# Where load tiles start in SBUF, one product per denominator, and a finer last load in a decode-attention kernel

## Chip, cores and metric

The kernel runs on one core of a Trainium2 chip. The metric is device time in microseconds, median of several executions. A ratio is the mean time of one kernel's fast runs over that of the kernel before in the same rounds on the same chip, so not quite the ratio of the medians beside it; its interval is 95%. "The span's time" counts from the start of the profiled span, which is about 2 us shorter than the device time.

In profile lines, PE is TensorE's products and PEld its weight loads, DVE is VectorE, ACT ScalarE, POOL GpSimd, SPq the queue that issues the loads, DMA the 16 transfer engines. A timeline line gives start, duration, engine, source line (L), operation, out<-in, and in brackets the idle time before it and what ended it. A packet is one piece of a load, moved by one transfer engine. A stream of packets is called flat when they all take the usual shortest time, and a packet raised when it takes a little more.

## The reference, cut to what matters

A decode step: one token for each of two batch entries, layer-normed, goes through sliding-window attention (16 query heads on 8 key/value heads, window 4096, head size 256) and a small dense block with a mish activation; both are added to the input.

```python
W = min(4096, max(256, Sk // 4))                      # 4096 of 32768 positions
q = (x @ wq).reshape(B, Sq, Hq, Dh).transpose(0, 2, 1, 3)
k = repeat(k_cache[:, :, Sk - W:, :], rep, axis=1)    # rep = 2
v = repeat(v_cache[:, :, Sk - W:, :], rep, axis=1)
p = softmax(einsum("bhqd,bhkd->bhqk", q, k) * Dh ** -0.5)
o = einsum("bhqk,bhkd->bhqd", p, v)
return x + o.reshape(B, Sq, Hq * Dh) @ wo + mish_block(xn, w1, b1, w2)
```

There are 16 pairs of key/value head and batch entry. For each, 2 MiB of keys and 2 MiB of values are read once; all loads are 77.66 MB.

## The kernel before

The pools stand in SBUF in the order in which they are opened, so what `consts` holds sets where the load tiles start:

```python
consts = ctx.enter_context(tc.tile_pool(name="consts", bufs=1))
wo_pool = ctx.enter_context(tc.tile_pool(name="wo", bufs=3))
k_pool = ctx.enter_context(tc.tile_pool(name="kk", bufs=4))
v_pool = ctx.enter_context(tc.tile_pool(name="vv", bufs=5))
kt_pool = ctx.enter_context(tc.tile_pool(name="kt", bufs=3))
```

In the built program every tile of wo, k, v and kt starts 352 bytes past a multiple of 512. A key or value tile takes 16,384 contiguous bytes per partition. The denominators, and the main loop:

```python
def turn_p(s):                       # transpose the probabilities of step s; two steps per pair
    ...
    den = ps_den.tile([P, rep], FP32, tag="den", name="den")
    for n in range(NH):              # NH = 2
        nc.tensor.matmul(den[:], lhsT=rs[:, n : n + 1].to_broadcast([P, P]),
                         rhs=hsel[:], start=(n == 0), stop=(n == NH - 1))
    nc.vector.reciprocal(out=state["rec", i][:], in_=den[:])
...
for i in range(NK + KA):             # NK = 16 pairs, values two pairs behind
    if i + 2 < NK: load_k(i + 2)
    if i < NK:
        load_v(i, parts=1 if i < NK - 1 else 2)
        ...                          # load_wo at every second pair
        for half in range(NH):
            turn(s + 1)              # VectorE transposes keys into kt
            scores(s)                # TensorE products, ScalarE exp
            turn_p(s - 1)
    ...
    if i >= KA: values(i - KA)       # and mix(), the output product, at every second pair
```

The softmax here doesn't subtract the row's maximum and nothing guards it: scores larger than these inputs give would overflow.

## Time and profile before

| | before |
|---|---|
| device time, median | 194.75 us (194.56 to 195.1, 4 runs) |
| span profiled | 192.7 us |
| first load's data begins, last load's data ends | 1.79 and 187.87 us of the span |
| data packets' time per transfer engine (sum over 16) | 184.75 us |

The page shows one thing full: the transfer engines. The lines that say so, and those of the tail, stand in the prediction. The last two rows of the table come from the trace's records of single packets (start, duration, bytes). The sum (184.75) and the distance between first and last (186.08) are nearly equal: the stream has hardly a hole, so its length follows the sum of the packets. The sum is a mean over 16 engines, and the slowest of them ends later than the mean.

### The profile page before, as it was taken

How to read it: one execution, taken by the hardware profiler on the slowest of the kernel's cores; microseconds unless marked ns; L12 is line 12 of the kernel's file. 1: busy time of each engine (PE TensorE's matmuls, PEld its weight loads, DVE VectorE, ACT ScalarE, POOL GpSimd, SP SyncE). 2: the span in 40 equal slices, each digit the busy share in tenths (PEclk: the TensorE clock that was granted, in tenths of full speed). 3: DMA queues.
4: the chain of work that ended last, by engine and by line, in shares of the span. 5: the costliest groups of instructions: out<-in, count | busy, mean ns of one | idle time of the engine just before them, and what ended most of it. 6: DMA issues, size and time to landing. Idle time of an engine off the chain costs nothing.

```text
span 192.7 us, 3810 instructions
## 1 busy us (share of the span) xinstructions
PE 130.4 (68%) x1624; PEld 81.3 (42%) x1624; DVE 102.2 (53%) x137; ACT 25.5 (13%) x69; POOL 24.8 (13%) x138
## 2 busy tenths in 40 slices
PE   0242993999827985499709881797449592898854
PEld 0142381466513654246504651364324452364752
DVE  4605506996638390929264753838091744748101
ACT  5000110112200211012200220021101110021100
POOL 7004320022110112002200210020200200000000
PEclk9999996699995799669975998599957979589965
DMA  6999999999999999999999999999999999999960
GB/s 211 424 447 408 427 427 435 428 435 402 431 422 428 425 415 428 435 418 414 429 425 432 420 416 430 428 425 411 428 432 428 403 434 422 432 414 429 410 253 2
DMA packets 7674, 77.90 MB, mean 404 GB/s; under 512 B 741, under 2 KB 2793, under 8 KB 3050
## 3 DMA queue, kind: packets, MB, share of 16 engines
q1 hardware_dynamic: 7652, 77.66, 96.1%
q8 instruction: 12, 0.20, 0.4%
q14 instruction: 4, 0.03, 0.0%
q10 hardware_dynamic: 6, 0.01, 0.0%
HBM read 77.67 MB, written 0.00 MB: 403 GB/s over the span
## 4 chain that ended last, share of the span: by engine, by line
DMA 96%; PE 1%; SPq 1%; issue 0%; ACT 0%; DVE 0%
DMA v<-in_A_v_cache_dram 51%; DMA k<-in_A_k_cache_dram 18%; DMA wo<-in_A_wo_dram 17%; DMA v<-in_B_w_dram 10%; PE psA L201 1%; PE o L411 1%; SPq L109 0%; SPq L325 0%; ACT res L484 0%; DVE oT L422 0%; SPq L336 0%
## 5 line engine op out<-in xcount | busy, mean ns | idle before, releaser
L352 DVE STREAM_TRANSPOSE kt<-k 128x2048 f32<-128x2048 f32 x32 | 73.5, 2300 | 48.9 <-DMA k<-in_A_k_cache_dram 48.9
L364 PE MATMUL sc<-kt,qdiag 128*128 128x512 bf16 x256 | 75.0, 443 | 14.4 <-DVE kt L352 14.3
L364 PEld LDWEIGHTS <-qdiag 128*128 128x128 bf16 x256 | 26.1, 111 | 50.5 <-issue 24.1
L374 ACT ACTIVATE p<-sc 128x512 bf16<-128x512 f32 x32 | 19.1, 597 | 144.8 <-PE sc L364 140.9
L244 POOL COPY qdiag<-qrep 32x8 bf16<-32x8 bf16 x128 | 21.0, 186 | 125.3 <-PE sc L364 109.8
L201 PE MATMUL psA<-wo,oT 128*2 128x224 bf16 x64 | 12.5, 370 | 31.3 <-DVE oT L422 31.3
L411 PEld LDWEIGHTS <-v 128*128 128x128 bf16 x1024 | 27.9, 97 | 6.3 <-DMA v<-in_A_v_cache_dram 3.0
L411 PE MATMUL o<-pT,v 128*128 128x2 bf16 x1024 | 28.1, 163 | 2.7 <-DMA v<-in_A_v_cache_dram 2.7
L385 DVE STREAM_TRANSPOSE pT<-p 128x512 bf16<-128x512 bf16 x32 | 21.4, 671 | 0.0
L201 PEld LDWEIGHTS <-oT 128*2 128x2 bf16 x64 | 6.5, 111 | 34.6 <-DVE oT L422 32.0
L393 PEld LDWEIGHTS den<-hsel,rs 128*128 128x128 f32 x64 | 11.7, 227 | 3.8 <-issue 2.1
L401 DVE RECIPROCAL rec<-den 128x2 f32<-128x2 f32 x16 | 2.5, 153 | 18.7 <-PE den L393 18.7
L393 PE MATMUL den<-hsel,rs 128*128 128x2 f32 x64 | 9.4, 252 | 0.0
L215 PE MATMUL qT_ps<-xs,v 128*128 128x4 bf16 x112 | 3.3, 166 | 6.1 <-DMA v<-in_A_wq_dram 6.1
L422 DVE TENSOR_TENSOR oT<-o,rec 128x4 bf16<-128x4 f32 x16 | 2.1, 134 | 8.5 <-PE o L411 8.5
L374 ACT ACTIVATION_READ_ACCUMULATOR p<-sc 128x1 f32 x32 | 6.2, 194 | 0.0
L215 PEld LDWEIGHTS <-v 128*128 128x128 bf16 x112 | 3.1, 104 | 6.6 <-DMA v<-in_A_wq_dram 6.6
L224 DVE CAST qT<-qT_ps 128x64 bf16<-128x64 f32 x1 | 0.2, 225 | 7.0 <-PE qT_ps L215 7.0
L169 PE MATMUL xnT_ps<-ident,xn_bf 2*128 2x2 bf16 x7 | 0.5, 166 | 5.0 <-DVE xn_bf L133 5.0
L270 PE MATMUL hT_ps<-xs,v 128*128 128x4 bf16 x49 | 3.7, 195 | 0.0
L270 PEld LDWEIGHTS <-v 128*128 128x128 bf16 x49 | 3.2, 149 | 0.3
L201 PE MATMUL psA<-v,act_bf 128*2 128x224 bf16 x28 | 2.8, 259 | 0.0
(40 smaller groups left out, 22.5 us busy)
## 6 DMA issues: line engine op xcount, KB each, us to landing
k<-in_A_k_cache_dram SPq DMA_DIRECT2D x16, 2048.0 KB, 32.5
v<-in_A_v_cache_dram SPq DMA_DIRECT2D x15, 2048.0 KB, 34.8
v<-in_B_w_dram SPq DMA_DIRECT2D x2, 1568.0 KB, 21.2
wo<-in_A_wo_dram SPq DMA_DIRECT2D x7, 448.0 KB, 31.8
v<-in_A_wq_dram SPq DMA_DIRECT2D x1, 2048.0 KB, 7.8
v<-in_A_v_cache_dram SPq DMA_DIRECT2D x2, 1024.0 KB, 29.9
v<-in_A_wq_dram SPq DMA_DIRECT2D x1, 1536.0 KB, 11.1
wo<-in_A_wo_dram SPq DMA_DIRECT2D x2, 224.0 KB, 24.1
```

What stands on the lines that cost most here:

```text
L201: nc.tensor.matmul(psA[n][:, :], lhsT=lhsT, rhs=rhs, skip_group_check=True, **flags)
L215: nc.tensor.matmul(qT_ps[:, hh, e, :], lhsT=wq_v[s][:, hh, e, :], rhs=xs[:, s, :, :].rearrange("p x b -> p (x b)"), start=(s == 0), stop=( ...
L244: nc.gpsimd.tensor_copy(out=tv[rows, :, e, j * Q : j * Q + rep], in_=qrep[rows, :, h0 : h0 + rep, e, x, b],)
L270: nc.tensor.matmul(hT_ps[:, c, :, :].rearrange("p x b -> p (x b)"), lhsT=w1_v[:, s, c, :], rhs=xs[:, s, :, :].rearrange("p x b -> p (x b)" ...
L352: nc.vector.transpose(out=kt[:].bitcast(FP32), in_=k[:, half * TH * Dh : (half + 1) * TH * Dh].bitcast(FP32),)
L364: nc.tensor.matmul(psc[:], lhsT=qdiag[i % NW][:, n * NE + e, :], rhs=ktv[:, n, e, :, :], start=(n == 0 and e == 0), stop=(n == NB - 1 and ...
L374: nc.scalar.activation(out=p_sb[:], in_=psc[:].rearrange("p t c -> p (t c)"), func=ACT.Exp, scale=scale, accum_out=state["rs", i][:, s % N ...
L385: nc.vector.transpose(out=pT[:], in_=p_t.pop(s)[:])
L393: nc.tensor.matmul(den[:], lhsT=rs[:, n : n + 1].to_broadcast([P, P]), rhs=hsel[:], start=(n == 0), stop=(n == NH - 1),)
L401: nc.vector.reciprocal(out=state["rec", i][:], in_=den[:])
L411: nc.tensor.matmul(po[:, c, :], lhsT=vv[:, t, c, :], rhs=pTv[:, th, 0:rep], start=(t == 0 and c == 0), stop=(t == T - 1), skip_group_check ...
L422: nc.vector.tensor_tensor(out=oT[:, :, :, b], in0=po[:], in1=state.pop(("rec", i))[:].unsqueeze(1).to_broadcast([P, ND, rep]), op=ALU.mult,)
```

## The change

Its intent: load tiles at aligned addresses, less TensorE work per denominator, and less work behind the last landing. The diff, cut (the rest only renames):

```diff
-    consts = ctx.enter_context(tc.tile_pool(name="consts", bufs=1))
+    lead = ctx.enter_context(tc.tile_pool(name="lead", bufs=1))
+    ident = lead.tile([P, P], BF16)
+    hsel = lead.tile([P, Q], FP32)
     wo_pool = ...
     k_pool = ...
     v_pool = ...
     kt_pool = ...
+    consts = ctx.enter_context(tc.tile_pool(name="consts", bufs=1))
...
-        for n in range(NH):
-            nc.tensor.matmul(den[:], lhsT=rs[:, n : n + 1].to_broadcast([P, P]), rhs=hsel[:], ...)
+        sums = small.tile([P, rep], FP32, tag="sums", name="sums")
+        nc.vector.tensor_scalar(out=sums[:], in0=hsel, scalar1=rs[:, 0:1], scalar2=None, op0=ALU.mult)
+        nc.vector.scalar_tensor_tensor(
+            out=sums[:], in0=hsel, scalar=rs[:, 1:2], in1=sums[:], op0=ALU.mult, op1=ALU.add)
+        nc.tensor.matmul(den[:], lhsT=ones_f[:], rhs=sums[:], start=True, stop=True)
...
-            load_v(i, parts=1 if i < NK - 1 else 2)
+            load_v(i, (0, T) if i < NK - 1 else (0, T // 2, 3 * T // 4, T))
```

In the changed program wo, k, v and kt all start at multiples of 512.

More of the change, by code (lines that the diff above doesn't have):

```diff
@@ L110 @@
         wq_sb += [w[:, s, :] for s in range(hi - lo)]
-    ident = consts.tile([P, P], BF16)
     make_identity(nc, ident[:])
@@ L152 @@
             )
-    hsel = consts.tile([P, rep], FP32)
-    nc.vector.tensor_copy(out=hsel[:], in_=ident[:, 0:rep])
+    hsel = hsel[:, 0:rep]
+    nc.vector.tensor_copy(out=hsel, in_=ident[:, 0:rep])
     for j in range(1, NQ):
         nc.vector.tensor_tensor(
-            out=hsel[:], in0=hsel[:], in1=ident[:, j * Q : j * Q + rep], op=ALU.add
+            out=hsel, in0=hsel, in1=ident[:, j * Q : j * Q + rep], op=ALU.add
         )
+    ones_f = consts.tile([P, P], FP32)
+    nc.gpsimd.memset(ones_f[:], 1.0)
     NW = 3
@@ L328, in load_k, with load_v @@
         k_t[i] = t
-    def load_v(i, parts=1):
+    def load_v(i, cuts=(0, T)):
         kvh, b = heads[i]
@@ L333, in load_v @@
         vin = A_v_cache[b, kvh, s0:Sk, :].rearrange("(p t) d -> p t d", p=P)
-        for u in range(parts):
-            ts = slice(u * T // parts, (u + 1) * T // parts)
-            nc.sync.dma_start(out=t[:, ts, :], in_=vin[:, ts, :])
+        for lo, hi in zip(cuts, cuts[1:]):
+            nc.sync.dma_start(out=t[:, lo:hi, :], in_=vin[:, lo:hi, :])
         v_t[i] = t
@@ L390, in turn_p @@
         rs = state.pop(("rs", i))
-        den = ps_den.tile([P, rep], FP32, tag="den", name="den")
-        for n in range(NH):
-            nc.tensor.matmul(
-                den[:],
-                lhsT=rs[:, n : n + 1].to_broadcast([P, P]),
-                rhs=hsel[:],
-                start=(n == 0),
-                stop=(n == NH - 1),
-            )
+        sums = small.tile([P, rep], FP32, tag="sums", name="sums")
+        nc.vector.tensor_scalar(
+            out=sums[:], in0=hsel, scalar1=rs[:, 0:1], scalar2=None, op0=ALU.mult
+        )
+        nc.vector.scalar_tensor_tensor(
+            out=sums[:], in0=hsel, scalar=rs[:, 1:2], in1=sums[:], op0=ALU.mult, op1=ALU.add
+        )
+        den = ps_den.tile([P, rep], FP32, tag="den", name="den")
+        nc.tensor.matmul(den[:], lhsT=ones_f[:], rhs=sums[:], start=True, stop=True)
         state["rec", i] = small.tile([P, rep], FP32, tag="rec", name="rec", bufs=4)
```

## The prediction

Passages are cut from the recorded text, and marked there: what it told of the hardware without a trace or run of this case, and what it worked out from a transfer rate that did not come from this case (each packet's time over that rate, the upper bound of part 1, rival 1's packet time, rate and device time). The sum comes to 194.2 us. The 8 ns per packet in parts 1 and 3: the trace of before gives as much; two packets of 1,792 bytes take 2 x 74 = 148 ns where b1's one of 3,584 takes 140, and two of 6,272 take 2 x 239 = 478 where one of 12,544 takes 469 (medians). An estimate from the same trace, 230 ns for 6,272 bytes, leaves 9 ns over for b1's aligned packet, and 9 and 8 for the unaligned ones of 6,272 and 1,792 bytes.

> **What bounds the kernel now.** I read the page first: engine shares, the forty slices, the chain that ended last. Then the synchronisation queue's waits, the windows by stage, the last microseconds of the timeline, and the trace's single packet records (start, duration, bytes).
>
> From the page: engine busy shares, two rows of the slices, the chain by engine.
>
> ```profile
> PE 130.4 (68%) x1624; PEld 81.3 (42%) x1624; DVE 102.2 (53%) x137; ACT 25.5 (13%) x69; POOL 24.8 (13%) x138
> ...
> DMA  6999999999999999999999999999999999999960
> GB/s 211 424 447 408 427 427 435 428 435 402 431 422 428 425 415 428 435 418 414 429 425 432 420 416 430 428 425 411 428 432 428 403 434 422 432 414 429 410 253 2
> ...
> DMA 96%; PE 1%; SPq 1%; issue 0%; ACT 0%; DVE 0%
> ```
>
> No compute engine is over 68% busy, the transfer engines are full in 37 of 40 slices, and 96% of the chain is transfers. So the kernel is one stream of loads: 77.66 MB, with a short start and a short tail. The windows put numbers on the middle (start:end and us, busy time of PE, PEld, DVE, ACT, POOL, then granted clock, DMA share, GB/s):
>
> ```profile
> 60.00:120.00 60.00, 43.04 (x525) 25.80 (x523) 32.74 (x34) 8.26 (x24) 7.92 (x48) 0.84 1.01 424
> 120.00:180.00 60.00, 44.69 (x528) 26.74 (x528) 34.64 (x37) 8.26 (x24) 3.97 (x24) 0.81 1.01 424
> ```
>
> Both stages run at 424 GB/s with a DMA share of 1.01: no holes to fill. Only two things can shorten such a run: each packet takes less time, or the start or tail shrinks.
>
> Does compute hold the stream up? The queue's waits (queue and line, released by whom: us in total, times, longest):
>
> ```profile
> SPq L345 <- DMA v<-in_A_v_cache_dram: 30.3, 7, 5.8
> SPq L336 <- DMA k<-in_A_k_cache_dram: 27.2, 6, 4.7
> ...
> SPq L336 <- PE o L411: 0.4, 1, 0.4
> ```
>
> The issuing queue waits for earlier loads to land, and for the values product on PE 0.4 us once. A load is issued about 32 us before it lands (page, DMA issues), so even a wait of some microseconds for a buffer would not empty the queues.
>
> The tail, from the timeline (start us, duration us, what, idle before and releaser):
>
> ```profile
> 184.78 1.01 PE L411 MATMUL o<-pT,v 128*128 128x2 bf16 x32 [0.73 <-DMA v<-in_A_v_cache_dram]
> ...
> 187.26 1.01 PE L411 MATMUL o<-pT,v 128*128 128x2 bf16 x32 [1.47 <-DMA v<-in_A_v_cache_dram]
> 188.31 0.17 DVE L422 TENSOR_TENSOR oT<-o,rec 128x4 bf16<-128x4 f32 x1 [4.06 <-PE o L411]
> 188.53 1.65 PE L201 MATMUL psA<-wo,oT 128*2 128x224 bf16 x8 [0.26 <-DVE oT L422]
> ```
>
> The second half of the last values lands at about 187.2; then 32 products (1.01 us), the scaling, the output product (1.65 us), two copies and the store.
>
> [...] packets of 12,544 and 6,272 bytes have medians of 469 and 239 ns, so the extra 6,272 bytes cost 230 ns, 27.3 bytes per ns per engine. [...]
>
> **Part 1: aligned destinations.** In the built program before, every buffer of wo, k, v and kt starts 352 bytes past a multiple of 512; in the changed one all start at a multiple. Bytes and loads are the same. What can a packet gain? Packet medians [...]:
> - 16,384 bytes: median 613 ns, lowest common value 611[...].
> - 6,272 bytes: 239[...].
> - 1,792 bytes (half of wo's rows start 96 bytes past 512): 74[...].
> - The bias b1, one row of 3,584 bytes, whose tile lies at a multiple of 512 already (17,408): 140[...].
>
> This last line decides my view: **an aligned packet has the same 8 ns overhead as the unaligned ones**, and a 4-byte semaphore packet takes 9 ns in all. So the 8 ns look like the price of any packet. Also the whole load of the first key tile, unaligned, ran at 611, when the compute engines did little. What alignment may still touch is the spread above 611: 613 to 622 in most later loads and about a hundred packets above 640. Outside the first load, the 16,384-byte packets average about 618: 7 ns over, times 3,982 packets over 16 engines, 1.8 us. The rare packets of 1,000 ns and more come about once in three loads and look like memory, not alignment. I credit alignment with 0.3 us of the 1.8. [...]
>
> **Part 2: one product per denominator.** The two rows of the page (busy us, mean ns):
>
> ```profile
> L393 PEld LDWEIGHTS den<-hsel,rs 128*128 128x128 f32 x64 | 11.7, 227 | 3.8 <-issue 2.1
> L393 PE MATMUL den<-hsel,rs 128*128 128x2 f32 x64 | 9.4, 252 | 0.0
> L401 DVE RECIPROCAL rec<-den 128x2 f32<-128x2 f32 x16 | 2.5, 153 | 18.7 <-PE den L393 18.7
> ```
>
> Each f32 product shows as two records, so 64 are 32 products; 32 records remain. PE loses 4.7 us busy, PEld 5.8. DVE gains 32 small instructions; its 128x2 f32 tensor-tensor rows took 161 ns each, so about 5.2 us in all: 102 becomes 107 of 193 us. PE now waits for DVE's sums, behind a 0.67 us transposition; around 103 us that transposition ended 1.8 us before the products began, so mostly no wait. All of it lies beside the stream: worth **0**. The last denominator ended at 181.8, well before the last values. The new constant, a memset on POOL at the start, of 65 KB of f32 ones, should cost about 0.5 us (the 128x512 bf16 one took 0.52); POOL then idles 12.2 us before its next work, so 0 too.
>
> **Part 3: the last values in three loads** (a half, two quarters). All bytes arrive in the same order, so the last quarter lands when the last half did, but only 16 products wait for it: 0.5 of the 1.01 us goes. The output weights behind it don't take it back: by packet records their last semaphore is written at 187.9 in the span's time, with about 0.5 us from writing to release as for the values (186.7 written, 187.2 seen), so 188.3; the output product would start at 188.0 with the first half of the weights (0.57 us earlier) and reach the second at about 188.8. Cost: 128 more packets x 8 ns / 16 = 0.06 us. Net **-0.45 us**.
>
> **Sum.** 194.92 - 0.3 - 0 - 0.45 = 194.2 us.
>
> **Rivals.**
> 1. Alignment is the hidden price of every packet[...]. For it: the stream is all of the time, so anything per packet shows in full. Against it: b1's 140 ns. [...]
> 2. Alignment removes only the spread, if that comes from writes colliding with compute accesses. For it: the first key load is flat at 611 and later ones are not. Against it: the collisions need not depend on the offset. Up to 1.8 us: 192.7.
> 3. DVE in the denominator becomes a wait on PE, values are finished late, buffers come free late. Against it: 0.4 us of such waiting today, and 32 us of queue ahead. If PE lost 1 us per head, PE's busy and stalled time would be near 146 of 193 us, still hidden: 194.2 to 194.9.
> 4. The stream's end is set by the slowest of 16 engines: their last semaphores spread over 1.5 us. A few slow packets landing elsewhere moves the time by some tenths either way, as much as part 3 gains.
>
> **Range and chances.** The repeats of before spread 0.5 us (194.56 to 195.1), so upward I allow 195.1 (nothing gained, some skew). Downward rival 2 in full gives 192.7. Range 192.7 to 195.1. Faster by over 2% needs 191.0, which only rival 1 reaches: 0.06. Slower by over 2% needs a new hole in the stream: 0.01. Within 2%: 0.93.
>
> **What would show each step right or wrong.** Right: 16,384-byte packets still at 611 to 615 with the lowest value 611; both long windows at 424 to 427 GB/s; b1's packet, now 384 bytes past a multiple, still about 140 ns; the den rows at x32 with about 5 us each; DVE near 107 us; the last group of values products x16 and about 0.5 us long. Wrong: packets of 605 or less, or windows of 430 and over (rival 1); the packets above 611 gone (rival 2); slices below 9 in the DMA row or waits of the queue for PE of some microseconds (rival 3); a last values landing that moved by more than 0.5 us while packets did not (rival 4).

## The result, and the profile after

The changed kernel takes **192.74 us** (192.59 to 193.12, 4 runs) against 194.75; ratio 0.9898, interval 0.9875 to 0.9921. That is inside the stated range by 0.04 us, and the gain, 2.0 us, is over twice the 0.75 us that I had summed.

From the page of the changed kernel: the engines, the two stream rows, and the chain by engine.

```profile
PE 129.6 (68%) x1592; PEld 75.5 (39%) x1592; DVE 108.0 (57%) x169; ACT 25.5 (13%) x69; POOL 25.0 (13%) x139
...
DMA  6999999999999999999999999999999999999960
GB/s 216 422 440 420 434 428 432 432 424 420 432 432 436 425 418 432 429 425 421 440 429 436 414 429 427 429 436 422 436 432 429 412 438 425 429 423 438 402 259 2
...
DMA 82%; DVE 10%; PE 6%; SPq 0%; issue 0%; ACT 0%
```

And its two long windows (busy times of PE, PEld, DVE, ACT, POOL, then clock, DMA share, GB/s):

```profile
60.00:120.00 60.00, 41.16 (x511) 23.26 (x509) 35.76 (x47) 8.26 (x24) 7.91 (x48) 0.84 1.01 428
120.00:180.00 60.00, 45.47 (x460) 23.74 (x461) 35.76 (x48) 7.57 (x22) 3.95 (x24) 0.76 1.01 428
```

The same full row of nines now carries 428 GB/s instead of 424. A busy share cannot show this gain: the engines are as busy as before (a DMA share of 1.01 in both), but the packets are shorter (16,384 bytes: median 611 instead of 613 ns). The chain has also changed its end: DVE and PE have a part in it, which before was transfers alone. The last stretch of the changed kernel (start us, duration us, what, idle before):

```profile
176.49 3.49 PE L368 MATMUL sc<-kt,qdiag 128*128 128x512 bf16 x8
...
181.67 0.70 DVE L389 STREAM_TRANSPOSE pT<-p 128x512 bf16<-128x512 bf16 x1
...
182.52 0.22 DVE L399 SCALAR_TENSOR_TENSOR sums<-hsel,rs,sums 128x2 f32<-128x2 f32 x1
182.79 0.30 PEld L403 LDWEIGHTS den<-sums,ones_f 128*128 128x128 f32 x2 [0.32 <-DVE sums L399]
...
183.04 3.55 PE L415 MATMUL o<-pT,v 128*128 128x2 bf16 x128
...
186.84 1.65 PE L206 MATMUL psA<-wo,oT 128*2 128x224 bf16 x8 [0.26 <-DVE oT L426]
```

Where I had expected a group of 16 values products waiting for the last landing, 128 products run in one piece: PE came late, and the last values were there before it. The first line is one cause: from 176 to 180 us of this execution the granted clock was 0.53, and eight score products took 3.49 us. The other is the wait for the sums; both are weighed under e4.

The packet records say what became of the stream. "Excess" is the time above the packet's usual shortest duration (611 ns for 16,384 bytes, 74 for 1,792), summed and divided by the 16 engines; packets of the first 9 us are left out for the 16,384-byte ones.

| | before | after |
|---|---|---|
| 16,384 bytes: at or below 611 ns | 14% | 99% |
| 612 to 640 ns: excess | 84%, 0.85 us | 0.4%, 0.00 us |
| above 640 ns: number, excess | 107, 0.63 us | 12, 0.32 us |
| 1,792 bytes (wo): excess | 0.30 us | 0.06 us |
| all data packets per engine | 184.75 us | 183.32 us |
| last load's data ends | 187.87 us | 186.43 us |

The stream became 1.4 us shorter, nearly all of it by packets that no longer exceed 611 (and 74) ns. Of the 107 packets above 640 ns, about 90 follow directly on a packet of wo on the same engine, as far as the records tell.

### The profile page after: what moved, and what is told of

The parts are those of the page before. It is cut to its first block, busy times and chain, and to the rows that moved or that the text cites. A ratio compares the mean times of both kernels' runs of the same rounds, so it can differ in the third digit from the quotient of the medians.

```text
span 191.1 us, 3752 instructions
## 1 busy us (share of the span) xinstructions
PE 129.6 (68%) x1592; PEld 75.5 (39%) x1592; DVE 108.0 (57%) x169; ACT 25.5 (13%) x69; POOL 25.0 (13%) x139
## 4 chain that ended last, share of the span: by engine, by line
DMA 82%; DVE 10%; PE 6%; SPq 0%; issue 0%; ACT 0%
DMA k<-in_A_k_cache_dram 64%; DMA wo<-in_A_wo_dram 18%; DVE kt L356 7%; PE o L415 3%; DVE pT L389 2%; PE sc L368 2%; PE psA L206 1%; PE den L403 1%; SPq L113 0%; DVE sums L399 0%; DVE oT L426 0%; DVE sums L396 0%; ACT res L488 0%; SPq L330 0%
## 5 line engine op out<-in xcount | busy, mean ns | idle before, releaser
L368 PE MATMUL sc<-kt,qdiag 128*128 128x512 bf16 x256 | 77.6, 456 | 14.1 <-DVE kt L356 14.1
L368 PEld LDWEIGHTS <-qdiag 128*128 128x128 bf16 x256 | 27.3, 115 | 51.3 <-issue 29.1
L403 PE MATMUL den<-sums,ones_f 128*128 128x2 f32 x32 | 5.9, 254 | 12.0 <-DVE sums L399 12.0
L403 PEld LDWEIGHTS den<-sums,ones_f 128*128 128x128 f32 x32 | 5.9, 212 | 19.5 <-DVE sums L399 17.8
L399 DVE SCALAR_TENSOR_TENSOR sums<-hsel,rs,sums 128x2 f32<-128x2 f32 x16 | 3.5, 221 | 0.6
```

The lines of the kernel that those rows point to most:

```text
L368: nc.tensor.matmul(psc[:], lhsT=qdiag[i % NW][:, n * NE + e, :], rhs=ktv[:, n, e, :, :], start=(n == 0 and e == 0), stop=(n == NB - 1 and ...
L399: nc.vector.scalar_tensor_tensor(out=sums[:], in0=hsel, scalar=rs[:, 1:2], in1=sums[:], op0=ALU.mult, op1=ALU.add)
L403: nc.tensor.matmul(den[:], lhsT=ones_f[:], rhs=sums[:], start=True, stop=True)
```

## The experiments

Theory: where a load's destination starts decides the excess, the denominator gives part of the tail's gain back. Rivals: the lighter TensorE work or the new order of the pools cleaned the packets; compute accesses collide with loads.

### One part at a time

**e1_align**: the kernel before with the new pool order alone.

```diff
-    consts = ... (first pool)
+    lead = ... (ident, hsel), then wo, kk, vv, kt, then consts
```

> The pools in the new order, so wo, k, v and kt start at multiples of 512 bytes; two denominator products and two last loads as before. Theory (the offset of a load's destination makes packets slow): 16,384-byte packets all at 611 ns, mean excess of the stream gone, last data packet 1.4 us earlier than in the kernel before, time 193.3 us, ratio 0.992 to 0.994. Rival (the denominator's lighter use of PE, not the offset, cleaned the packets): packets stay at 611 to 622 and the ratio is 1.00.

Measured: 192.91 us against 194.76, ratio 0.9905 (0.9891 to 0.9918). 99% of the 16,384-byte packets at 611, last data at 186.45 us. **Alignment alone is worth 1.85 us**, 0.4 more than the theory had expected. The packets explain 1.4 to 1.5 of it; about 0.2 more is that the profiled run of before (194.53) was faster than its median, and I did not trace the rest.

**e2_den**: the kernel before with the one-product denominator alone.

```diff
-        two matmuls of rs with hsel
+        sums on VectorE, one matmul with ones_f
```

> The kernel before with the one-product denominator alone; loads still start 352 bytes past a multiple of 512. Theory: packets stay spread over 611 to 622 ns; the time is within 0.3 us of the kernel before, ratio 0.999 to 1.002; PE waits for the sums about 10 us in all. Rival (denominator cleaned the packets): packets at 611, ratio 0.993.

Measured: 194.74 against 194.76, ratio 0.9996 (0.9984 to 1.0009), 13% of the packets at 611. So the denominator neither cleaned the packets nor cost anything by itself. The waits of PE in this run (who waits for whom: us in total, times, longest) show that the new wait is there, but hidden:

```profile
PE den L401 <- DVE sums L397: 11.1, 7, 1.9
```

**e3_cuts**: the kernel before with the last values in three loads alone.

```diff
-            load_v(i, parts=1 if i < NK - 1 else 2)
+            load_v(i, (0, T) if i < NK - 1 else (0, T // 2, 3 * T // 4, T))
```

> The kernel before with the last values in three loads alone. Theory: packets spread as before, the last values products 16 instead of 32 behind the last landing, 0.45 us less, ratio 0.9975. Rival (PE or the output weights behind it take it back): ratio 1.000.

Measured: 194.40, ratio 0.9979 (0.9966 to 0.9993), 0.36 us less. Its tail:

```profile
187.41 0.59 PE L410 MATMUL o<-pT,v 128*128 128x2 bf16 x16 [0.68 <-DMA v<-in_A_v_cache_dram]
188.04 0.17 DVE L421 TENSOR_TENSOR oT<-o,rec 128x4 bf16<-128x4 f32 x1 [3.65 <-PE o L410]
188.26 1.65 PE L201 MATMUL psA<-wo,oT 128*2 128x224 bf16 x8 [0.26 <-DVE oT L421]
```

Sixteen products, 0.59 us, stand behind the landing, where 32 took 1.01; the output product follows at once, so the weights behind the values did not delay it.

**e4_align_cuts**: the changed kernel with the two denominator products of before, that is e1 and e3 together.

```diff
         (aligned pools, three last loads)
-        sums on VectorE, one matmul with ones_f
+        two matmuls of rs with hsel
```

> The changed kernel with the two denominator products of before: aligned loads and three last loads. Theory (waits of PE for the sums give part of the tail's gain back in the changed kernel): about 0.3 us under the changed kernel, ratio 0.988; in the tail PE waits for the last landing again. Rival (the tail's gain is lost to something else, such as the granted clock): same as the changed kernel, ratio 0.990.

Measured: 192.55 (192.52 to 192.71), ratio 0.9887 (0.9874 to 0.9901). The tail of this run:

```profile
175.09 1.91 PE L365 MATMUL sc<-kt,qdiag 128*128 128x512 bf16 x8 [0.52 <-DVE kt L353]
...
184.29 0.59 PE L412 MATMUL o<-pT,v 128*128 128x2 bf16 x16 [0.19 <-DMA v<-in_A_v_cache_dram]
185.53 0.59 PE L412 MATMUL o<-pT,v 128*128 128x2 bf16 x16 [0.65 <-DMA v<-in_A_v_cache_dram]
186.15 0.16 DVE L423 TENSOR_TENSOR oT<-o,rec 128x4 bf16<-128x4 f32 x1 [3.49 <-PE o L412]
186.37 1.65 PE L203 MATMUL psA<-wo,oT 128*2 128x224 bf16 x8 [0.26 <-DVE oT L423]
```

PE waits for the landing again, and the output product starts at 186.37 instead of 186.84, though the last data ended at nearly the same moment (186.35 against 186.43). So the changed kernel lost 0.4 us of the tail in its profiled run. The expectation named a rival for this, the granted clock, and the two profiles don't settle it. The last eight score products started 1.4 us later in the changed kernel (176.49 against 175.09), behind the wait for the sums, and then took 1.6 us longer (3.49 against 1.91), at a granted clock of 0.53 from 176 to 180 us, where this run had 1.00. In e2 the wait without the low clock stayed hidden (its stream ends later), and in best a low clock without the wait did (0.65 from 172 to 176 us). The two together are the likely cause; no run separates them. In the timed runs the difference is 0.2 us, and the two intervals overlap: two of the four runs of the changed kernel (192.59 and 192.6) lie among those of e4. That the denominator costs time in the median is not shown.

### Which offset, and whose

The next six start from e4 and insert padding ahead of a pool; nothing else changes.

**o32** and **o64**: 32 or 64 bytes ahead of all load tiles.

```diff
     hsel = lead.tile([P, Q], FP32)
+    lead.tile([P, 32 // 2], BF16, name="pad")     # o64: 64 // 2, o256: 256 // 2
```

> The aligned kernel with three last loads (192.55 us), with 32 bytes of padding ahead of the load tiles: wo, k, v and kt start 32 bytes past a multiple of 512, pools in the new order. Theory (the offset of the load's destination): the packets of 16,384 bytes spread over 612 to 622 again, about 1.4 us of excess, time near 194.2 us, ratio 0.9975. Rival (the order of the pools, not the offset): packets stay at 611 and the time at 192.55, ratio 0.989.

> The same with 64 bytes of padding: load tiles 64 bytes past a multiple of 512. Theory A (a multiple of 512 is needed): spread as at 32 bytes, ratio 0.9975. Theory B (a multiple of 64 is enough): packets at 611, ratio 0.989.

Measured: o32 194.85 us, ratio 1.0007 (0.9993 to 1.0022), packets 94% within 612 to 640, excess 1.7 us; o64 194.47, ratio 0.9987 (0.9972 to 1.0002), 90% within 612 to 640, excess 1.5 us. So it is the offset and not the pools' order, and a multiple of 64 is not enough. o32 was slower than expected by 0.6 us: against e4 its packets' sum grew by 1.77 us, but the last data came 2.20 us later (188.55), so the slowest engine lost more than the mean. What holds that engine up was not traced. The two long windows of o32 are back at the rate of before, one GB/s lower even:

```profile
60.00:120.00 60.00, 42.66 (x527) 25.46 (x524) 32.64 (x34) 8.25 (x24) 7.90 (x48) 0.84 1.01 423
120.00:180.00 60.00, 43.29 (x511) 25.56 (x512) 35.01 (x37) 8.25 (x24) 3.95 (x24) 0.81 1.01 423
```

**o256**: 256 bytes ahead of all load tiles. (For the excess of the output weights' rows see the table: 0.06 us over all 2,048 packets of wo in the changed kernel.)

> Load tiles 256 bytes past a multiple of 512, otherwise the aligned kernel with three last loads. Theory A (512 needed): packets of 16,384 spread, ratio 0.998. Theory B (256 is enough; half of the output weights' rows lie so in the aligned kernels and show no excess): 611, ratio 0.989.

Measured: 192.51, ratio 0.9885 (0.9868 to 0.9901), 99% at 611. **A multiple of 256 is enough**; 512, as the change has it, buys nothing more here. 128 was not tried.

**kt32**: load tiles at multiples of 512, only kt and what lies behind it 32 bytes off.

```diff
+    gap = ctx.enter_context(tc.tile_pool(name="gap", bufs=1))
+    gap.tile([P, 16], BF16, name="pad")
     kt_pool = ...
```

> The same with the padding behind the load tiles: wo, k and v at multiples of 512, only kt (written by the vector engine) and everything behind it 32 bytes off. Theory (the load's destination counts): packets at 611, ratio 0.989. Rival (compute engines' unaligned accesses to kt collide with the loads): packets spread, ratio 0.995 or more.

Measured: 192.58, ratio 0.9892 (0.9875 to 0.9908), 99% at 611. The offset of the tiles that VectorE and ScalarE write does not matter to the loads.

**v32** and **k32**: only the values' tiles, or only the keys' tiles, 32 bytes off.

```diff
     k_pool = ...
+    gap (32 bytes)        # v32; in k32 this stands ahead of k_pool
     v_pool = ...
+    gap2 (480 bytes)      # back to a multiple of 512; in k32 ahead of v_pool
```

> wo and k at multiples of 512, v (values, first weights, dense weights) 32 bytes off, kt back at a multiple. Theory (each packet pays for its own destination): packets into k stay at 611, those into v spread over 612 to 622; about half of the excess, ratio 0.993. Rival (one unaligned stream disturbs all 16 engines): packets into k spread too.

> The mirror of the run with only v off: k starts 32 bytes past a multiple of 512, v, wo and kt at multiples. Theory S[...]: packets at 611, as with only v off, ratio 0.989 to 0.991. Rival D (what hurts is k's offset itself, for instance the vector engine's reads of unaligned k): packets spread over 612 to 622, ratio 0.997.

Measured: v32 193.02, ratio 0.9913 (0.9898 to 0.9928), 96% at 611; k32 192.82, ratio 0.9902 (0.9887 to 0.9917), 97% at 611. v32 misses the simple theory (0.993 for packets that pay for their own destination), and k32 comes out as the theory S that I drew from v32 had said (packets at 611, 0.989 to 0.991). What S supposed inside a transfer engine is cut from the recorded texts, as no run shows it. Together they are the most telling result here. In v32 nearly all packets into v stay at 611 although they are unaligned; in o32 most packets into the very same addresses take 612 to 621. So **a packet does not pay for its own destination alone**. Nor do the compute engines' reads of either cause it alone: VectorE reads unaligned k in k32, TensorE unaligned v in v32, and both streams are nearly flat. v32 is still 0.47 us slower than e4: its packets' sum is the same (183.28 against 183.24), but its last data ended 0.32 us later (186.67). Why is open.

The packet records can be strung into chains, one per transfer engine, where a packet starts as another ends. Nanoseconds above 611 for successive 16,384-byte packets of one chain each ("|" where one load ends and the next begins):

```
o32:  8 2 3 10 3 3 3 10 | 1 2 10 3 3 3 10 3 | 1 10 3 3 3 10 3 3 | 8 2
v32:  0 0 0 0 0 0 0 0   | 0 0 0 0 0 0 0 0   | 0 0 0 0 0 0 0 0   | 0 0
k32:  3 10 3 | 1 10 3 3 3 10 3 3 | 8 0 0 0 0 0 0 0 | 0 0 0 0 0 0
```

In o32 the pattern repeats every four packets and does not end. In the k32 chain, the only one of that stretch that is not flat, it runs through two key loads (unaligned) and ends behind the first packet of the next values load (aligned). Another chain of k32 is raised at 98.6 us, flat for eight packets, and raised again from 104.1, so a flat stretch is not always the end. These patterns are what was measured; what makes them no run shows.

**even32**: all load tiles 32 bytes off as in o32, and every large packet's length and source start a multiple of 512 (w1 and w2 cut to 12,288 bytes per row, wo in rows of 3,584). It asks whether packets of odd length or start (12,544, 6,272 and 1,792 bytes) are what starts the spread; theory S took them for it. The 0.5 us expected from fewer packets is an estimate: 1,024 fewer of wo, at the 8 ns by which two of 1,792 bytes exceed one of 3,584 in the trace of before, over 16 engines.

```diff
-        nc.sync.dma_start(out=dense["w1"], in_=B_w1...)         # 12,544 bytes per row
+        nc.sync.dma_start(out=w1[:, 0:6144], in_=flat(B_w1))    # 12,288; w2 likewise
-        win = A_wo[...]"(h p c) d -> p h (c d)"                 # 1,792 bytes
+        win = flat rows of A_wo                                 # 3,584 bytes
```

> All load tiles 32 bytes off as in the run of that offset, which was spread; but every packet but the tiny ones has a length and a source start that are multiples of 512 bytes: the dense weights are cut to 12,288 bytes per row and the output weights come in rows of 3,584. The result is wrong on purpose. Theory S[...]: packets of 16,384 stay at 611 although all destinations are unaligned. Rival (an unaligned destination is slow by itself once the stream is busy): 612 to 622 again. The time is then no measure of alignment alone, as fewer packets save some 0.5 us: 192.1 under S, 193.6 under the rival.

Measured: 194.37, 0.8 us above even the rival's figure, with 96% of the 16,384-byte packets within 612 to 640. Odd lengths are not what starts the spread. They do go with its longest packets: 11 exceed 640 ns here, 104 in o32. In this run as in o32 packets are flat up to 18 us of the span, and by 21 to 22 us they exceed their shortest duration by 4 ns or more on average. **What starts it stays open**, but the records hold one hint. In k32, about two thirds of the raised packets lie within 24 packets behind a packet of the instruction queue in the same chain, and such stretches hold only 6% of all packets (v32: a third, in 6%). So raised packets gather behind a packet of another queue; that it starts them is a guess. They do not only begin there: in even32 the chain with such a packet is raised first, at 18.9 us, and the other 15 follow by 20.9 us without one. No run tested it.

### A better version

**best**: e4 with the last values in four loads. (The 0.06 us expected for 128 more packets is the forecast's 8 ns each, over 16 engines.)

```diff
-            ... (0, T // 2, 3 * T // 4, T)
+            ... (0, T // 2, 3 * T // 4, 7 * T // 8, T)
```

> The aligned kernel with the two denominator products of before and four last loads (half, quarter, two eighths). Only 8 values products wait for the last landing instead of 16: 0.25 us less, 0.06 us given back to 128 more packets; 192.35 us, ratio 0.9875. Rival (the output weights, which land last, now bound the tail): 192.55.

Measured: 192.48 (192.45 to 192.54), ratio 0.9883 (0.9869 to 0.9898): no different from e4's 192.55. The output product starts at 186.37 here as there. The 8 last products take 0.37 instead of 0.59 us, but began at 185.74 instead of 185.53, so the finer cut gained nothing. e4, o256, kt32 and best (192.48 to 192.58) are the fastest, and equal within the noise; each keeps the two denominator products.

## Why the prediction was right or wrong

- **The bound** was right: a full stream whose length is the sum of its packets, so only packet time, start or tail could move it. The 2 us came from there. That the time still fell inside the range, by 0.04 us, was partly luck: the same alignment and cuts with the old denominator (e4, 192.55) lie below its end of 192.7.
- **Part 1, the sum's first term, was mis-sized.** "I credit alignment with 0.3 us of the 1.8": it measured 1.85 us alone. The 1.8 itself was a little high: these packets average 616.9 ns, not 618, so 1.48 us lay above 611, and the change left 0.32 of it. What failed was the argument for dividing it. I took b1's 140 ns and the flat first key load as proof that unaligned packets cost no more. The first stands: the usual shortest time is the same aligned and unaligned (611 remains 611, and b1 kept 140 ns at its new offset of 384). The second does not: an unaligned stream can run flat for a time and then not: in o32 it is flat up to 18 us of the span, and yet 94% of all its packets take 612 to 640 ns.
- **"The rare packets of 1,000 ns and more ... look like memory"** was wrong for most, though harmless. In the trace of before, 10 of the 12 load packets of 16,384 bytes and 1,000 ns or more start as a packet of the same size of the instruction queue ends: one of these lasts from 36.92 to 37.94 us, and the load packet from 37.92 takes 1,158 ns. The other two have no such neighbour. Alignment leaves them: 8 of the 12 packets above 640 ns after the change stand so, with 0.25 of the remaining 0.32 us.
- **Rival 2** named the right effect and size ("alignment removes only the spread", 192.7), and its own sign came true: the packets above 611 are gone. Its cause, collisions with compute accesses, is not what the runs show (kt32, v32, k32). **Rival 1** was rightly refused: packets did not drop below 611, their median after the change.
- **Part 2** was right alone: e2 gives 0. PE's busy time for the products fell to 5.9 us (4.7 foreseen), PEld's to 5.9 as foreseen, VectorE rose to 108.0 (107 foreseen), and the ones took 0.2 us (0.5 foreseen). But "mostly no wait" was wrong: PE waited behind half of the 16 denominators. In the changed kernel:

```profile
PE den L403 <- DVE sums L399: 12.0, 8, 1.8
```

  It stays hidden while PE waits for loads anyway (e2). In the changed kernel's profiled run PE no longer waited for the last landing, by this wait and a low clock together.
- **Part 3** was right: 0.45 foreseen, 0.36 measured alone. The parts measured alone add to 2.23 us (1.85 + 0.02 + 0.36), the whole is 2.0; the whole's interval reaches from about 1.5 to 2.4 us, so a loss where the parts meet is possible but not shown.
- **Rival 3** expected that this wait would free buffers late and found it hidden; it is, in the stream. In the tail, where no rival looked, it was part of what made PE late. **Rival 4**: the last data moved by 1.44 us, the packets' sum by 1.43, so a shifted slowest engine has no part in it (in o32 and v32 it has).

## What to carry to other kernels

Where the transfer row is full of nines, compare GB/s and single packet durations, not busy shares: here 424 became 428 GB/s at a DMA share of 1.01 in both, and of the 1.48 us that the 16,384-byte packets took above their usual shortest time 1.16 were to be had. Start tiles that loads fill at multiples of 256 bytes, all of them: in o256 99% of the 16,384-byte packets took 611 ns and the kernel 192.51 us; 32 or 64 bytes off, 94 and 90% took 612 to 640 ns and the kernel 194.85 and 194.47 us; with only v or only k 32 bytes off it took 193.02 and 192.82. Build a variant that shifts them by 32 to learn what it is worth. In the changed kernel's profiled run a wait that e2 had hidden behind the stream (11.1 us there, 12.0 here) came out in the tail, together with a low clock, when the stream's end had moved forward by 1.4 us; so price changes near the tail together. And before one profile's tail is put down to an edit, compare the granted clock there (0.53 against 1.00 here).
